# Interleaved token order, two wide stores a step, mirrored x rows gathered by GpSimd, x loaded three steps ahead

## The chip, the core and the metric

The kernel runs on one core of a Trainium2 chip. A core has five engines with queues of their own: PE (TensorE, matmuls; its weight loads are listed as PEld), DVE (VectorE), ACT (ScalarE), POOL (GpSimd) and SP (SyncE, which here only issues DMA transfers). Each engine takes its instructions in order. DMA transfers can be issued from the queues of SP, ACT and POOL. The metric is the device time of one launch, in microseconds (us).

## The reference

What is computed is a Fourier mixing layer (the real part of a 2-D Fourier transform over the 3136 tokens and 256 features), and then a mixer with a low-rank token path and a two-layer channel path:

```python
X = fft(fft(x, axis=1), axis=2).real          # x: 8 x 3136 x 256, float32
h = X.transpose(0, 2, 1) @ U @ V              # U: 3136 x 32, V: 32 x 3136
u = X + h.transpose(0, 2, 1)
out = u + maximum(u @ w_ch1, 0) @ w_ch2       # w_ch1: 256 x 1024, w_ch2: 1024 x 256
```

## The kernel before

The eight batch entries are worked as four pairs. The 3136 tokens are written as n = 64 n1 + n2 on the way in (49 by 64) and as k = 49 k2 + k1 on the way out. Since the input is real, output token k and its mirror are computed together, and so are feature d and 256 - d; only k1 = 0 to 24 is worked, and a mirrored line comes from the same products.

**The input side** of a pair (classes `load_steps`, `s1_steps`): x comes in eight chunks c. `load_pair_chunk` (L96) issues two transfers per chunk from SP's queue: `xa`, 98 rows (2 entries by 49 values of n1) of 4 lines each, and `xb` (L107), the mirrored lines, whose 49 rows of an entry are read in descending order (an access pattern with a negative step, outermost dimension 2). `fold_pair_chunk` (L151, L152) adds the two on POOL into `y`; `fold_pair_chunk_d` and `fold_d` (L141 to L143) fold the features, with two DVE instructions and a small copy of the two edge columns on ACT, into `yb`. Two steps of stage 1 per chunk (L194) multiply `yb` by a table `F`; the result is copied to `z` by ACT and every fourth step stored to DRAM (`zturn`, L206). At the end of the eight chunks `turn` (L274) reads `zturn` back into `g` with another axis on the partitions. `te_steps`, `te_turn`, `te_hidden` and `te_direct` work out the low-rank path (tiles `te`, `TT`, `TE`, `TK`).

**The output side.** `lines` makes eight lines of 64 tokens of one entry from `g` (tile `q`, up to 512 columns at a time); the one row of them that the low-rank product needs is copied into `VZ` by a 1 KB transfer (L383). A pair has 13 chunks of output: 12 with 256 token columns and a mini chunk. A chunk has two steps, so a pair has 26. Per step there are two calls of `mlp1` (L425 and L432 on PE, a copy `ab` on ACT at L435, and two DVE instructions, L438 and L441, that make the hidden tile `hT` and its mirrored twin) for the current chunk, and one `mlp2` with two phases for the chunk before (L480 and the smaller L490 on PE). After the first phase stands a no-operation on ACT (`st.turn`, L492), for which the first matmul of the second phase waits: the two phases write the two halves of a PSUM tile in turned roles. `drain` (L511) copies the result to `om` on ACT, adds and subtracts its halves on POOL into `ob` (L522, L523), and stores `ob` with four transfers of 64 rows of 1 KB (L527).

**The order** is written out by hand in `plan`. `at[n]` holds what is issued in step n of a pair, behind the step's matmuls and ahead of its `drain`. `place_next` places the input side of the next pair: chunk c is loaded at step a + gap c, folded on POOL two steps later, on DVE four, and its stage 1 comes five steps later. `a` and `gap` are 4 and 1.75 in pair 0, and 0 and 2.3 in pairs 1 and 2. Pair 3 has no successor to prepare. Pair 0 also works its own second entry (`turned_steps`, `te_single`) and the tables that are left (`product`, `pair_tables`, `v_lines`, `v_copy`).

**Buffers:** `xa` and `xb` three each, `y` two, `yb` three, `ob` four, `om` three; PSUM has four tiles of two banks, shared by all.

Of the kernel before, what the change touches and what calls it, by code (L numbers as in the profile page):

```python
# [22 lines left out]
def kernel(  # L23
# [19 lines left out]
    ud = nc.dram_tensor("uturn", (NK1, 2, 32, 64), BF16, kind="Internal").ap()  # L43
    x_pn = x.rearrange("b (n1 n2) d -> (b n1) n2 d", n2=N2)
# [28 lines left out]
    sgm = cpool.tile([P, 2], FP32, name="sgm")  # L73
    sg = cpool.tile([P, 2], FP32)
# [21 lines left out]
    def load_pair_chunk(p, c):  # L96
# [10 lines left out]
        nc.sync.dma_start(out=ck.xb.rearrange("p l d -> p (l d)"),  # L107
                          in_=bass.AP(x.tensor, x.offset + r * 4 * D, [[N1 * 64 * D, 2], [-64 * D, N1], [1, 4 * D]]))
# [30 lines left out]
    def fold_d(yb, src, l0, l1):  # L139
        o, i = yb[:, l0:l1, :], src[:, l0:l1, :]  # L140
        nc.vector.tensor_tensor(o[:, :, 1:128], i[:, :, 1:128], i[:, :, 255:128:-1], op=AL.add)  # L141
        nc.vector.tensor_tensor(o[:, :, 129:256], i[:, :, 1:128], i[:, :, 255:128:-1], op=AL.subtract)  # L142
        nc.scalar.copy(o[:, :, 0:129:128], i[:, :, 0:129:128])  # L143
# [32 lines left out]
    def s1_steps(pr, evac):  # L176
# [5 lines left out]
        def step(g):  # L182
# [20 lines left out]
            if g % 4 == 3:  # L203
                lo = max(30 - 2 * g - 1, 0)
                hi = 37 - 2 * g
                nc.sync.dma_start(out=zdp[:, lo:hi, :], in_=z[:, lo:hi, :])  # L206
                if g == 15:
                    nc.sync.dma_start(out=zdp[:, 31, :], in_=z[:, 31, :])
# [76 lines left out]
    def te_turn(pr, bs):  # L285
# [5 lines left out]
        for i, b in enumerate(bs):  # L291
# [3 lines left out]
            copy_act(o[:, :, 64:96], src)  # L295
# [59 lines left out]
    def lines(pr, b, c, evac, now=False):  # L355
# [3 lines left out]
        if now:  # L359
            ps[1] = bank2("ln")  # L360
# [10 lines left out]
    def lines_out(q, ps, b, c, evac, now):  # L371
        c0 = b * 1536 + 512 * c
        o = q[:, :, c0:c0 + 512].rearrange("p k (i s j) -> p s k i j", i=4, s=2)
# [3 lines left out]
        for s in range(2) if now else []:  # L377
            evac[s](o[:, s], ps[s][:, s].rearrange("p (k i j) -> p k i j", k=2, i=4))
            if now:
                evac[s](zr.rearrange("p (i s j) -> p s i j", i=4, s=2)[:, s],  # L380
                        ps[s][64:65, s, 0:256].rearrange("p (i j) -> p i j", i=4))
        if not now:
            nc.sync.dma_start(out=zr, in_=q[64:65, 0, c0:c0 + 512])  # L383
# [27 lines left out]
    def mlp1_parts(ch, u):  # L411
        q, c0, w = ch.pr.q, ch.c0, ch.w
        m = 512 // w
        if u == 0:
            ch.h = hpool.tile([P, 2, JT, 256], BF16, tag="h", name="hT")
# [11 lines left out]
        yield  # L427
        for i in range(m):
# [10 lines left out]
        if not ch.mini:  # L439
            flip = [v.rearrange("p i (t n) -> p (i t) n", n=P) for v in [h[:, 0], a, b]]  # L440
            nc.vector.tensor_tensor(flip[0][:, :, ::-1], flip[1], flip[2], op=AL.max)  # L441
            if u == 0:
# [11 lines left out]
    def mlp2(ch, t, mixed):  # L454
# [56 lines left out]
        def drain(eng):  # L511
# [12 lines left out]
            for i in range(n):  # L524
                for hf, (b, k) in enumerate(ch.units[t]):
                    r = slice(64 - 64 * hf, 128 - 64 * hf) if i else slice(64 * hf, 64 * hf + 64)
                    nc.sync.dma_start(out=out[b].rearrange("(k2 k1) d -> k1 k2 d", k1=N1)[N1 - k if i else k], in_=ob[r, i])  # L527
# [78 lines left out]
    nc.sync.dma_start(out=VZ[96:97].rearrange("p b j -> p (b j)").rearrange("p (a j) -> p a j", j=640), in_=idle[0:5])  # L606
# [119 lines left out]
    nc.gpsimd.memset(V0[:].bitcast(FP32), 0.0)  # L726
    gate = tmp([64, 4], "gate")
# [49 lines left out]
    def v_lines(eng, k0, k1):  # L777
        for r, op in [(0, AL.add), (64, AL.subtract)]:
            o = VZ[r:r + 32, 0, 64 * k0:64 * k1].rearrange("p (k j) -> p k j", j=64)
            eng.tensor_tensor(o, Vk[r:r + 32, k0:k1, :], Vk[r:r + 32, N1 - k0:N1 - k1:-1, ::-1], op=op)  # L780
# [7 lines left out]
    def v_copy(k0, k1, first=True):  # L788
# [29 lines left out]
    bp_sin()  # L818
    te_single(first, 0, teps)
    lps = lines(first, 0, 0, None, now=True)  # L820
    te_turn(first, [0])
    lps([copy_act, copy_dve])
    w1ps = bank2("w1ps")
    w1_fold(1, w1ps)
    te_hidden(first, 0, 0)
    nc.scalar.mul(W1p[1][:], w1ps[:], 0.5)
# [3 lines left out]
    v_copy(1, 9)  # L830
    loads = load_single(1)
# [12 lines left out]
    pairs = [first] + [Pair(p) for p in range(1, NP)]  # L844
    chunks = [ch for p in range(NP) for ch in pair_chunks(p)]
# [12 lines left out]
    def product():  # L858
        ps = bank2("w12")
        for blk in range(2):  # L860
            for j in range(JT):
                nc.tensor.matmul(ps[:, blk, 0:D], W1T[:, j // 4, blk, (j % 4) * P:(j % 4 + 1) * P], W2[:, j, :],
                                 start=(j == 0), stop=(j == JT - 1))
        m = ps[:, :, 0:D]

        copy_act(G[:], m)
        nc.gpsimd.memset(RR[0][0:64].bitcast(FP32), 0.0)
# [164 lines left out]
```

## Time and profile before

| | us |
|---|---|
| median of 2 runs (613.95 to 617.14) | 615.55 |
| the profiled execution | 616.54 |
| its span, first to last instruction | 614.3 |
| PE busy in the span | 485.0 (79%) |
| DVE / ACT / POOL busy | 356.6 / 279.0 / 249.4 |
| mean granted clock of TensorE | 0.875 of full speed |
| moved by DMA | 65.53 MB, 107 GB/s over the span |

In a row of a group, behind the bar, stand the busy time in total and the mean of one instruction in ns, and then the idle time of the engine right before such instructions with what ended it. In a row of a waits view stand the total, the number and the longest of the waits. In a row of a timeline stand start, duration, engine, line and operation, and in brackets the idle time before. In a row of a windows view stand the stretch, its length, the busy time of PE, PEld, DVE, ACT and POOL with the number of instructions, the granted clock, the busy share of the 16 DMA engines and GB/s. In a row of one line's instructions stand the shortest, the median and the longest duration in ns.

### The profile page before, as it was taken

How to read it: one execution, taken by the hardware profiler on the slowest of the kernel's cores; microseconds unless marked ns; L12 is line 12 of the kernel's file. 1: busy time of each engine (PE TensorE's matmuls, PEld its weight loads, DVE VectorE, ACT ScalarE, POOL GpSimd, SP SyncE). 2: the span in 40 equal slices, each digit the busy share in tenths (PEclk: the TensorE clock that was granted, in tenths of full speed). 3: DMA queues.
4: the chain of work that ended last, by engine and by line, in shares of the span. 5: the costliest groups of instructions: out<-in, count | busy, mean ns of one | idle time of the engine just before them, and what ended most of it. 6: DMA issues, size and time to landing. Idle time of an engine off the chain costs nothing. (4 is left out here: it accounts for less than half of the span.)

```text
span 614.3 us, 19104 instructions
## 1 busy us (share of the span) xinstructions
PE 485.0 (79%) x8159; PEld 384.2 (63%) x8159; DVE 356.6 (58%) x592; ACT 279.0 (45%) x505; POOL 249.4 (41%) x342
## 2 busy tenths in 40 slices
PE   4788798294869798886584979878677498999995
PEld 3658575183758476674462847756456285888894
DVE  7567894253764376564465337746456545676673
ACT  5665344152633455353342345534334235656552
POOL 7285334633451234444535124453453512333340
PEclk9788997686978798797795879988869589999998
DMA  8571334444338324334342832443434282233333
GB/s 158 172 106 25 88 110 108 133 117 137 102 109 180 82 91 121 124 100 128 96 126 64 174 88 90 118 130 95 128 93 126 63 180 67 56 75 71 73 80 79
DMA packets 60751, 65.53 MB, mean 107 GB/s; under 512 B 13593, under 2 KB 53496, under 8 KB 60504
## 3 DMA queue, kind: packets, MB, share of 16 engines
q1 hardware_dynamic: 56426, 59.45, 37.2%
q0 software_dynamic: 4160, 4.66, 4.3%
q8 instruction: 63, 1.03, 0.7%
q10 hardware_dynamic: 80, 0.20, 0.1%
q14 instruction: 22, 0.18, 0.1%
HBM read 34.62 MB, written 32.19 MB: 109 GB/s over the span
## 5 line engine op out<-in xcount | busy, mean ns | idle before, releaser
L480 PE MATMUL ops<-W,hT 64*128 64x256 bf16 x3072 | 224.7, 287 | 48.4 <-ACTq L492 41.3
L438 DVE SCALAR_TENSOR_TENSOR hT<-ab,hps 128x512 bf16<-128x512 bf16 x200 | 136.6, 683 | 172.3 <-ACT ab L435 172.2
L480 PEld LDWEIGHTS <-hT 64*128 64x128 bf16 x3072 | 158.9, 100 | 85.7 <-ACTq L492 44.6
L435 ACT CAST ab<-hps 128x512 bf16<-128x512 f32 x200 | 117.0, 590 | 127.1 <-PE hps L432 107.1
L425 PE MATMUL hps<-q,W1p 64*128 64x256 bf16 (+1 forms) x1248 | 131.3, 281 | 13.0 <-DVE hT L441 11.2
L151 POOL TENSOR_TENSOR y<-xa,xb 98x510 f32<-98x510 f32 (+1 forms) x48 | 58.1, 1231 | 192.6 <-DMA xb<-in_x_dram 184.1
L522 POOL TENSOR_TENSOR ob<-om 128x256 f32<-128x256 f32 (+1 forms) x97 | 78.0, 804 | 142.5 <-ACT om L521 121.3
L441 DVE TENSOR_TENSOR hT<-hps,ab 128x512 bf16<-128x512 f32 x192 | 130.8, 681 | 0.0
L425 PE MATMUL hps<-q,W1z 64*128 64x256 bf16 (+1 forms) x416 | 106.3, 282 | 0.0
L432 PE MATMUL hps<-VZ,TE 33*128 33x256 bf16 (+1 forms) x896 | 84.5, 273 | 27.4 <-DMA VZ<-q 27.1
L425 PEld LDWEIGHTS <-W1p 64*128 64x128 bf16 x1248 | 72.9, 99 | 31.0 <-DVE hT L441 19.4
L523 POOL TENSOR_TENSOR ob<-om 128x256 f32<-128x256 f32 (+1 forms) x97 | 78.2, 806 | 0.0
L141 DVE TENSOR_TENSOR yb<-y 98x508 bf16<-98x508 f32 (+1 forms) x24 | 33.8, 1409 | 62.7 <-POOL y L151 62.6
L432 PEld LDWEIGHTS <-TE 33*128 33x128 bf16 x896 | 44.4, 100 | 34.7 <-issue 28.4
L521 ACT COPY om<-ops 128x512 f32<-128x512 f32 (+1 forms) x97 | 56.4, 581 | 9.9 <-PE ops L490 9.8
L490 PE MATMUL ops<-TK,VS 64*128 64x256 f16 x192 | 54.6, 284 | 0.5 <-ACT TK L80 0.5
L425 PEld LDWEIGHTS <-W1z 64*128 64x128 bf16 x416 | 41.0, 99 | 3.0 <-issue 2.1
L490 PEld LDWEIGHTS <-qr 64*128 64x128 bf16 x384 | 38.2, 100 | 3.6 <-issue 0.4
L143 ACT CAST yb<-y 98x8 bf16<-98x8 f32 (+1 forms) x24 | 5.5, 227 | 76.9 <-POOL y L152 76.9
L490 PEld LDWEIGHTS <-q 64*128 64x128 bf16 x384 | 38.2, 100 | 2.8
L490 PE MATMUL ops<-R,qr 64*128 64x256 f16 x192 | 38.9, 284 | 0.0
L490 PE MATMUL ops<-R,q 64*128 64x256 f16 x192 | 38.8, 284 | 0.0
(181 smaller groups left out, 483.0 us busy)
## 6 DMA issues: line engine op xcount, KB each, us to landing
out_dram<-ob SPq DMA_DIRECT2D x392, 64.0 KB
xa<-in_x_dram SPq DMA_DIRECT2D x24, 392.0 KB
xb<-in_x_dram SPq DMA_DIRECT2D x24, 392.0 KB
zturn<-z SPq DMA_DIRECT2D x9, 512.0 KB
g<-zturn SPq DMA_DIRECT2D x6, 416.0 KB
g<-zturn SPq DMA_DIRECT2D x6, 384.0 KB
X<-in_x_dram POOLq DMA_DIRECT2D x4, 384.0 KB, 8.1
X<-in_x_dram POOLq DMA_DIRECT2D x2, 744.0 KB, 8.1
```

Source lines behind the costliest of these rows:

```text
L141: nc.vector.tensor_tensor(o[:, :, 1:128], i[:, :, 1:128], i[:, :, 255:128:-1], op=AL.add)
L151: nc.gpsimd.tensor_tensor(ck.y[:, l0:l1, 1:256], ck.xa[:, l0:l1, 1:256], rb[:, l0:l1, 255:0:-1], op=AL.add)
L425: nc.tensor.matmul(o[s], lt, q[64 * s:64 * s + 64, blk, c0:c0 + w], start=(i == 0 and blk == 0), stop=True, skip_group_check=True)
L432: nc.tensor.matmul(ps[:, s, i * w + a:i * w + a + n], TE[ch.p % 2][b][64 * s:64 * s + 33, ja], VZ[64 * s:64 * s + 33, b, v:v + n], start=F ...
L435: nc.scalar.copy(ab[:], ps[:, 1])
L438: nc.vector.scalar_tensor_tensor(h[:, 1], b, -1.0, a, op0=AL.mult, op1=AL.max)
L441: nc.vector.tensor_tensor(flip[0][:, :, ::-1], flip[1], flip[2], op=AL.max)
L480: mm = nc.tensor.matmul(op, ch.h[rows[half], s, j, t * P:(t + 1) * P], W2[rows[half], j, :], start=(ha == 0 and j == 0), stop=False, skip_ ...
L490: last = nc.tensor.matmul(*g[k], start=False, stop=(k == len(g) - 1), skip_group_check=True)
L521: nc.scalar.copy(om, po)
L522: eng.tensor_tensor(ob[:, 0:n, 0:P], a, om[:, :, 1], op=AL.add)
L523: eng.tensor_tensor(ob[:, 0:n, P:D], a, om[:, :, 1], op=AL.subtract)
```

## The change

- **Token order.** The two lines of a 128-column group are interleaved, token by token, in `q`, `VZ` and the V tiles. The 128 partitions of `ob` are then 64 pairs of neighbouring output rows, and `drain` stores each half of `ob` with one transfer of 128 rows (runs of 2 KB in DRAM): two a step instead of four. The mini chunk stays as it was.
- **xb** is gathered by an indirect DMA from POOL's queue, one row index per partition; the indices are an iota plus an offset, made once.
- **Queues.** `zturn` stores and the `VZ` row transfers are issued from ACT's queue. The edge copy of `fold_d` goes from ACT to DVE.
- **Order.** In `place_next` fold, DVE fold and stage 1 stand one step further behind the load (3, 5, 6); `a` is 3 in pair 0, `gap` 2.25 in pairs 1 and 2.
- **Start.** The first halves of chunk 0's two `mlp1` calls are issued in the preparation. `product` adds the table `Bp` by two matmuls with the identity instead of on DVE; its rows 0 to 63 are filled by POOL and ACT at step 0 (`product_rows`). `v_lines` and `v_zero` all come at step 0, `v_copy`'s mirrored copies go from DVE to ACT. The zero row of `VZ` is a POOL memset instead of a transfer. The copy `qr` is made one `mlp1` call later, and the tile `hT` is taken after the call's first matmuls.

```diff
+    x_g = x.rearrange("b (n1 g l) d -> (b n1 g) (l d)", g=16, l=4)
...
-        r = 2 * p * N1 * 16 + 48 * 16 + 15 - c
-        nc.sync.dma_start(out=ck.xb.rearrange("p l d -> p (l d)"),
-                          in_=bass.AP(x.tensor, x.offset + r * 4 * D, [[N1 * 64 * D, 2], [-64 * D, N1], [1, 4 * D]]))
+        nc.gpsimd.indirect_dma_start(
+            out=ck.xb.rearrange("p l d -> p (l d)"), out_offset=None, in_=x_g,
+            in_offset=bass.IndirectOffsetOnAxis(ap=idx[:, 8 * p + c:8 * p + c + 1], axis=0))
...
-        nc.scalar.copy(o[:, :, 0:129:128], i[:, :, 0:129:128])
+        nc.vector.tensor_copy(o[:, :, 0:129:128], i[:, :, 0:129:128])
...
-                nc.sync.dma_start(out=zdp[:, lo:hi, :], in_=z[:, lo:hi, :])
+                nc.scalar.dma_start(out=zdp[:, lo:hi, :], in_=z[:, lo:hi, :])
                 if g == 15:
-                    nc.sync.dma_start(out=zdp[:, 31, :], in_=z[:, 31, :])
+                    nc.scalar.dma_start(out=zdp[:, 31, :], in_=z[:, 31, :])
...
-        o = q[:, :, c0:c0 + 512].rearrange("p k (i s j) -> p s k i j", i=4, s=2)
+        o = q[:, :, c0:c0 + 512].rearrange("p k (i j s) -> p s k i j", i=4, s=2)
...
-            nc.sync.dma_start(out=zr, in_=q[64:65, 0, c0:c0 + 512])
+            nc.scalar.dma_start(out=zr, in_=q[64:65, 0, c0:c0 + 512])
...
-            for i in range(n):
+            rows = out.rearrange("b (k2 k1) d -> b k2 k1 d", k1=N1)
+            if ch.mini:
                 for hf, (b, k) in enumerate(ch.units[t]):
-                    r = slice(64 - 64 * hf, 128 - 64 * hf) if i else slice(64 * hf, 64 * hf + 64)
-                    nc.sync.dma_start(out=out[b].rearrange("(k2 k1) d -> k1 k2 d", k1=N1)[N1 - k if i else k], in_=ob[r, i])
+                    nc.sync.dma_start(out=rows[b, :, k], in_=ob[64 * hf:64 * hf + 64, 0])
+            else:
+                b, k = ch.units[t][0]
+                for i, k in enumerate([k, N1 - k - 1]):
+                    nc.sync.dma_start(out=rows[b, :, k:k + 2], in_=ob[:, i])
...
-    nc.sync.dma_start(out=VZ[96:97].rearrange("p b j -> p (b j)").rearrange("p (a j) -> p a j", j=640), in_=idle[0:5])
...
+    nc.gpsimd.memset(VZ[96:97].bitcast(FP32), 0.0)
...
-            o = VZ[r:r + 32, 0, 64 * k0:64 * k1].rearrange("p (k j) -> p k j", j=64)
-            eng.tensor_tensor(o, Vk[r:r + 32, k0:k1, :], Vk[r:r + 32, N1 - k0:N1 - k1:-1, ::-1], op=op)
+            o = VZ[r:r + 32, 0, 64 * k0:64 * k1].rearrange("p (i j s) -> p s i j", j=64, s=2)
+            for s in range(2):
+                eng.tensor_tensor(o[:, s], Vk[r:r + 32, k0 + s:k1:2, :], Vk[r:r + 32, N1 - k0 - s:N1 - k1:-2, ::-1], op=op)
...
-            copy_dve(v2[1][0:32, :, ::-1], v2[0][0:32])
-            ts(v2[1][32:64, :, ::-1], v2[0][32:64], -1.0, None)
+            copy_act(v2[1][0:32, :, ::-1], v2[0][0:32])
+            nc.scalar.mul(v2[1][32:64, :, ::-1], v2[0][32:64], -1.0)
...
+    first.u = [mlp1_parts(ch0, i) for i in range(2)]
+    next(first.u[0])
     te_hidden(first, 0, 0)
+    next(first.u[1])
...
+    idx0 = cpool.tile([PR, 8 * NP], I32, name="idx0")
+    nc.gpsimd.iota(idx0[:], pattern=[[PR * 16, NP], [-1, 8]], base=48 * 16 + 15, channel_multiplier=-16)
...
-                                 start=(j == 0), stop=(j == JT - 1))
+                                 start=(j == 0), stop=False, skip_group_check=True)
+        for blk in range(2):
+            nc.tensor.matmul(ps[:, blk, blk * P:(blk + 1) * P], eye[:], Bp[:, blk], start=False, stop=True, skip_group_check=True)
...
-            nc.vector.tensor_tensor(G[:, blk, o], G[:, blk, o], Bp[:, blk], op=AL.add)
-            nc.vector.tensor_tensor(RR[0][64:P, blk, o], RR[0][64:P, blk, o], Bp[64:P, blk], op=AL.add)
-            nc.vector.tensor_copy(RR[0][0:64, blk, o], Bp[0:64, blk])
-            nc.vector.tensor_copy(RR[1][0:64, blk, o], Bp[0:64, blk])
...
-                for o, f in [(0, load), (2, fn), (4, fd), (5, s1[2 * c]), (5, s1[2 * c + 1])]:
+                for o, f in [(0, load), (3, fn), (5, fd), (6, s1[2 * c]), (6, s1[2 * c + 1])]:
                     at[int(a + gap * c) + o].append(f)
-            e = int(a + gap * 7) + 5
+            e = int(a + gap * 7) + 6
...
-            place_next(pairs[1], 4, 1.75)
+            place_next(pairs[1], 3, 1.75)
...
-                place_next(pairs[p + 1], 0, 2.3)
+                place_next(pairs[p + 1], 0, 2.25)
```

More of the change, by code (lines that the diff above doesn't have):

```diff
@@ L73 @@
     sgm = cpool.tile([P, 2], FP32, name="sgm")
+    idx = cpool.tile([PR, 8 * NP], I32)
     sg = cpool.tile([P, 2], FP32)
@@ L427, in mlp1_parts @@
         yield
+        if u == 0:
+            ch.h = hpool.tile([P, 2, JT, 256], BF16, tag="h", name="hT")
         for i in range(m):
@@ L842 @@
     apool = ctx.enter_context(tc.tile_pool(name="apool", bufs=2))
-    pairs = [first] + [Pair(p) for p in range(1, NP)]
-    chunks = [ch for p in range(NP) for ch in pair_chunks(p)]
     NCK = len(chunks) // NP
@@ L985 @@
             n = 2 * (i % NCK) + t
+            if i + t == 0:
+                for g in first.u:
+                    next(g)
+                us_ = []
             if len(us_) == 2:
```

46 lines of the change are left out of this document (26 added, 20 removed).

## The prediction

> **What bounds the kernel now.** I read the busy time by stage first: the windows view, cut at the first matmul of the loop (33.3 us) and at the mini chunk's plain matmuls that close each of the four pairs (206.1, 359, 511.7 and 606.2 us).
>
> ```profile
> core 0: us, PE busy (x) PEld busy (x) DVE busy (x) ACT busy (x) POOL busy (x), PEclk, DMA share, GB/s
> 33.30:94.00 60.70, 50.63 (x991) 41.70 (x992) 47.11 (x101) 29.61 (x55) 31.74 (x44) 0.94 0.39 85
> 94.00:188.00 94.00, 65.80 (x923) 50.80 (x921) 47.86 (x69) 36.64 (x69) 40.83 (x50) 0.78 0.43 121
> 188.00:206.10 18.10, 14.75 (x326) 11.91 (x321) 5.29 (x10) 7.45 (x15) 5.62 (x8) 0.96 0.74 145
> 206.10:359.00 152.90, 119.37 (x1878) 91.14 (x1878) 85.21 (x119) 65.13 (x120) 61.30 (x74) 0.85 0.42 111
> 359.00:511.70 152.70, 119.67 (x1882) 90.96 (x1879) 84.87 (x119) 65.05 (x120) 61.32 (x74) 0.86 0.42 111
> 511.70:606.20 94.50, 91.62 (x1744) 81.57 (x1742) 63.45 (x100) 54.48 (x95) 31.82 (x46) 1.00 0.31 70
> 606.20:614.30 8.10, 1.55 (x12) 0.81 (x10) 1.46 (x5) 0.64 (x2) 0.00 (x0) 0.78 0.36 82
> ```
>
> The last pair prepares no successor: 94.5 us, PE busy for 91.6 of them at clock 1.00, so PE bounds it. Its 26 steps take 94.5/26 = 3.63 us each, a matmul 94.5/1744 = 54 ns. Pairs 1 and 2 issue only 134 more matmuls but take 152.8 us at a clock of 0.85. At 54 ns those would be 7 us; the other 50 us per pair are waiting and the lower clock. What is waited for stands in the groups and the waits (SP's own last):
>
> ```profile
> L480 PE MATMUL ops<-W,hT 64*128 64x256 bf16 x3072 | 224.7, 287 | 48.4 <-ACTq L492 41.3 <-DVE hT L441 5.3 <-DVE hT L438 0.6
> L432 PE MATMUL hps<-VZ,TE 33*128 33x256 bf16 (+1 forms) x896 | 84.5, 273 | 27.4 <-DMA VZ<-q 27.1 <-issue 0.2
> L143 ACT CAST yb<-y 98x8 bf16<-98x8 f32 (+1 forms) x24 | 5.5, 227 | 76.9 <-POOL y L152 76.9
> L151 POOL TENSOR_TENSOR y<-xa,xb 98x510 f32<-98x510 f32 (+1 forms) x48 | 58.1, 1231 | 192.6 <-DMA xb<-in_x_dram 184.1 <-DMA out_dram<-ob 5.8 <-DVE yb L142 2.7
> SPq L527 <- POOL ob L523: 101.9, 46, 12.3
> SPq L527 <- DMA xb<-in_x_dram: 81.3, 18, 5.9
> ```
>
> Read upward, this is one chain. POOL's fold waits 184 us for xb; ACT's edge copy waits for the fold; ACT works in order, so its "bank turn" nop (L492) is late and PE waits 41 us for that. SP's stores, queued behind, wait for xb's transfer too. The timeline of one such stop, and the DMA in its middle:
>
> ```profile
> 107.71 0.57 SPq L103 DMA_DIRECT2D xa<-in_x_dram  x1
> 108.32 0.69 SPq L107 DMA_DIRECT2D xb<-in_x_dram  x1
> 114.68 0.57 SPq L383 DMA_DIRECT2D VZ<-q  x1
> 119.20 2.48 POOL L151 TENSOR_TENSOR y<-xa,xb 98x510 f32<-98x510 f32 x2 [5.55 <-DMA xb<-in_x_dram]
> 120.08 0.61 PE L432 MATMUL hps<-VZ,TE 33*128 33x256 bf16 x4 [11.64 <-DMA VZ<-q]
> ```
>
> ```profile
> 108.40:110.60 2.20, 0.04 (x2) 0.00 (x0) 0.68 (x1) 1.06 (x3) 2.20 (x4) 1.00 0.74 210
> 110.60:111.80 1.20, 0.00 (x0) 0.00 (x0) 1.20 (x2) 0.17 (x1) 1.20 (x2) 1.00 0.13 44
> ```
>
> xa and xb are both 98 rows of 4 KB, 401 KB. For 2.2 us the DMA moves 210 GB/s (462 KB: xa and a start of xb); then only xb is left, at 44 GB/s and a share of 0.13, two of sixteen engines. 401 KB at 44 GB/s are 9.1 us; xb is in use 10.9 us after its issue. The 1 KB row VZ<-q, issued at 114.68, lands 5.4 us later, just when xb is done: it stands behind xb.
>
> **The change, part by part.** *The gather of xb.* One transfer of SP on two engines becomes 98 rows that POOL fetches by index. If they spread as xa's rows do, 401 KB need about 2 us; even the 10.9 us of now would fit in three steps of 3.63 us, which is what the earlier load gives. So I let the 184 us of fold waits go and ask what is late next: the load cycle, 2.25 steps per chunk of x, on the engines it shares.
>
> ```profile
> L438 DVE SCALAR_TENSOR_TENSOR hT<-ab,hps 128x512 bf16<-128x512 bf16 x200 | 136.6, 683 | 172.3 <-ACT ab L435 172.2
> L441 DVE TENSOR_TENSOR hT<-hps,ab 128x512 bf16<-128x512 f32 x192 | 130.8, 681 | 0.0
> L523 POOL TENSOR_TENSOR ob<-om 128x256 f32<-128x256 f32 x94 | 76.8, 817 | 0.0
> L522 POOL TENSOR_TENSOR ob<-om 128x256 f32<-128x256 f32 x94 | 76.6, 815 | 121.9 <-ACT om L521 100.7 <-DMA out_dram<-ob 13.4 <-issue 7.8
> L141 DVE TENSOR_TENSOR yb<-y 98x508 bf16<-98x508 f32 x21 | 25.4, 1208 | 40.5 <-POOL y L151 40.5
> L142 DVE TENSOR_TENSOR yb<-y 98x508 bf16<-98x508 f32 x21 | 23.2, 1105 | 0.0
> L152 POOL TENSOR_TENSOR y<-xa,xb 98x4 f32<-98x4 f32 x21 | 4.4, 210 | 0.0
> L120 POOL DMA_DIRECT2D X<-in_x_dram x6 | 4.1, 685 | 0.3 <-POOL X L114 0.3
> L725 POOL MEMSET TT<- 1x1 bf16 x4 | 0.4, 104 | 0.2
> L780 POOL TENSOR_TENSOR VZ<-uv 32x512 bf16<-32x512 f32 x4 | 8.5, 2122 | 0.1
> 229.20:238.30 9.10, 8.57 (x152) 7.04 (x150) 7.43 (x11) 5.42 (x10) 6.25 (x8) 1.00 0.42 107
> 259.70:271.00 11.30, 9.53 (x177) 7.57 (x173) 8.15 (x12) 6.51 (x12) 7.63 (x9) 1.00 0.41 105
> ```
>
> DVE per cycle: two hT pairs a step, 2.25 x 2 x (0.683 + 0.681) = 6.14, the fold 1.208 + 1.105, and the edge copy that comes over from ACT (0.23 there, I take 0.2): 8.65 us. POOL: drains 2.25 x (0.817 + 0.815) = 3.67, folds 2 x 1.231 + 0.21 = 2.67, and the gather. The trace has no gather. Below stands a plain POOL DMA issue, 0.685; above, 98 indices at the price of POOL's smallest instruction, 98 x 0.104 = 10.2. Nearest is the plain issue, with the index work at the rate of the scattered L780 (2.122/512 = 4.1 ns an element, 0.4 us): 1.1 us, POOL 7.4 us. PE: 2.25 steps x 66 matmuls and 4 of stage 1, 152.5 x 54 ns = 8.2 us. Three engines at 85% and more do not mesh perfectly. The windows of pair 1 hold two stretches at clock 1.00 in which loads, folds and chunks ran nearly unhindered: 152 matmuls in 9.1 us, 177 in 11.3 (9.7 per 152.5). I take their mean, 9.4 us a cycle, with 8.65 and 11.4 as ends (11.4: see the POOL rival).
>
> Pairs 1 and 2: 8 cycles, 75.2; the 8 steps left, 29.1; the about 98 matmuls more than in the last pair that the cycles do not hold (te, lines, turn) at 54 ns, 5.3: 109.6 us each.
>
> *What leaves SP and ACT.* VZ<-q and zturn go to ACT's queue, L143 to DVE. ACT then waits neither for the fold nor, through it, for x; the 41 and 27 us of PE waits go with them (they lie inside the numbers above). The price is 23 + 12 + 3 issues on ACT:
>
> ```profile
> L383 SPq DMA_DIRECT2D VZ<-q x23: 519/554/1187, 37.7 to 564.6; - x23
> L206 SPq DMA_DIRECT2D zturn<-z x12: 532/535/1561, 115.3 to 491.7; - x12
> L527 SPq DMA_DIRECT2D out_dram<-ob x392: 466/594/1925, 54.0 to 611.0; - x196
> 605.91 5.71 SPq L527 DMA_DIRECT2D out_dram<-ob  x9
> ```
>
> At 0.55 us each that is some 7 us a pair on an ACT busy 65 of then 110 us: covered, but each delays the next ab by half a microsecond, and hT, hence PE, waits on ab; without cover up to 7 us a pair (in the upper end). [...] The row of 114.68 shows the queue at work: the issue took 0.57 us, the landing 5.4; but with xb off two engines even a VZ<-q left on SP would land soon, so the sum does not hang on it.
>
> *Stores.* 392 of 64 rows become 200 (192 of 128 rows, 8 mini ones). SP spends 0.594 us on each, 233 us in all; at the same price 119, at double 238, which SP can bear: its stops were waits. At the end the nine stores of 5.7 us become about five: 2 us off the 8.1 (0 to 3).
>
> *Start and pair 0.* The first halves of chunk 0 move forward (about 1 us); the product's additions move from DVE into PE, and the negations of v_copy from DVE to ACT:
>
> ```profile
> 44.88 0.28 PE L315 MATMUL tk<-G,TT 128*32 128x256 f16 x1 [1.69 <-DVE G L873]
> 45.99 0.27 PE L315 MATMUL tk<-G,TT 128*32 128x256 f16 x1 [0.83 <-DVE G L873]
> L555 DVE TENSOR_SCALAR VS<-VS 32x512 bf16<-32x512 bf16 x3 | 3.0, 1010 | 0.1
> ```
>
> That is 2.5 us of PE waiting and 3 us of DVE in a stretch (33.3 to 94) where DVE is busy 78%: with the first item 6.5, so 54 for 60.7. v_lines moves to step 0 as eight half-size POOL instructions, 8.5 us as before, ahead of the first drain: nothing. 94 to 188: 923 matmuls at a cycle's rate (152.5 per 9.4) are 57 for 94. The last 18.1 stay; they hold g's reload, which gets no faster. Pair 0: 129. The interleaved columns of q, VZ and V change strides, not element counts: nothing, at most 10% of a few 1 us copies. The VZ memset, iota and index additions are under 2 us each beside other work.
>
> *Sum:* 33.3 + 129 + 2 x 109.6 + 94.5 + 6.1 = 482 us of span. The profiled execution took 616.54 with a span of 614.3, 2.2 more; so 484. That execution lies 1.0 us above the median of the runs, 615.55; I take that off: **483**.
>
> **The rivals.** *POOL becomes the bound.* The gather is worked out on POOL, beside a DVE that is busier than before. If the gather takes 5 us, POOL's cycle is 3.67 + 2.67 + 5 = 11.4; 24 cycles 2 us longer give 483 + 48 = 531. For it: no row has a gather, and POOL has the least slack of the three. Against: the plain issues, of about as many bytes, cost 0.685. [...]
>
> *ACT takes SP's place.* If a zturn store on ACT is held by full queues as SP's stores were (at most 5.9 us, the SP row above), 12 of them stop ab, hT and PE for 71 us: 554. Against: what filled the queues was xb. For: g's reload keeps a DMA share of 0.74 around it.
>
> *The gather lands no sooner,* because mirrored rows, not two engines, make xb slow. Then it does not do what it says; but with 9.1 us per xb, three ahead and SP free of it, the cycle is still max(9.4, 9.1), with some folds late: about 495. Against: the share of 0.13.
>
> *Slower.* POOL is held for each index, 10.2 us a gather: cycle 16.5, 24 x 7.1 = 170 more: 653. It decides from a cycle of 14.9 (24 x 5.5 = 132 more), a gather of 8.6 us. For it only L725's price per instruction; against it the 0.685.
>
> **How the numbers follow.** Forecast 0.73, POOL 0.09, ACT 0.09, no sooner 0.05, slower 0.03, no change 0.01. Range: the low end is the cycle at 8.65, 24 x 0.75 = 18 less: 465; the high end takes in the gather landing no sooner and reaches POOL's 531: 465 to 531. Faster by over 2% (what a measurement of this kernel can tell) in all but the last two cases: 0.96; same 0.01, slower 0.03.
>
> **What would show it.** L151 with next to no wait for xb; L480 none for ACTq; L432 little for VZ<-q; pairs 1 and 2 near 110 us at clock 0.95 or more; POOL's gathers near 1.1 us; the last pair still 94 us. Wrong would be: gathers over 3 us, L435 or L521 late behind ACT's issues, or a DVE that holds PE for more than 10 us a pair.

## The result, and the profile after

The changed kernel takes **543.14 us** (median of 2 runs, 541.07 to 545.22) where the kernel before takes 615.55: a ratio of 0.8824, with a 95% interval of 0.8649 to 0.8999. The direction was forecast, the size was not: 483 us were predicted, and the range ended at 531. The profiled execution took 545.22 us with a span of 543.4, so the prediction's own sum, 482 us of span, is missed by 61. In the ratios here and below, runs at a clearly lower granted clock are left out, so a ratio is not always the quotient of two medians.

The windows view of the changed kernel, cut as before at the first matmul of the MLP and at the plain matmuls that close each pair (the first halves of two `mlp1` calls now stand ahead of the loop, so the first cut comes earlier):

```profile
core 0: us, PE busy (x) PEld busy (x) DVE busy (x) ACT busy (x) POOL busy (x), PEclk, DMA share, GB/s
...
31.00:181.60 150.60, 126.83 (x2235) 101.03 (x2234) 101.31 (x182) 80.66 (x140) 87.85 (x113) 0.91 0.50 127
181.60:307.30 125.70, 106.25 (x1881) 87.74 (x1879) 84.55 (x128) 67.08 (x112) 67.34 (x82) 0.97 0.46 135
307.30:435.70 128.40, 108.27 (x1881) 88.53 (x1880) 84.75 (x128) 67.28 (x112) 67.09 (x82) 0.96 0.46 132
435.70:537.00 101.30, 92.72 (x1744) 85.15 (x1742) 63.60 (x100) 56.68 (x96) 33.28 (x48) 0.98 0.21 67
```

Every pair is longer than forecast: pair 0 ends at 181.6 us (162 forecast), pairs 1 and 2 take 125.7 and 128.4 (109.6), and pair 3, which loads nothing at all, takes 101.3 where it took 94.5 before. That last one says that the missing time cannot lie in the loads alone. The groups on the page of the same kernel:

```profile
L480 PE MATMUL ops<-W,hT 64*128 64x256 bf16 x3072 | 214.8, 277 | 13.0 <-DVE hT L441 8.5
...
L423 PE MATMUL hps<-q,W1p 64*128 64x256 bf16 (+1 forms) x1248 | 132.1, 276 | 41.7 <-ACT q L82 27.4
...
L432 PE MATMUL hps<-VZ,TE 33*128 33x256 bf16 (+1 forms) x896 | 82.7, 267 | 0.6 <-ACT TE L82 0.6
...
L153 POOL TENSOR_TENSOR y<-xa,xb 98x510 f32<-98x510 f32 (+1 forms) x48 | 58.1, 1229 | 2.4 <-DVE yb L145 2.4
```

What was to go has gone: POOL's fold (L153) waited 184 us for xb and now waits for nothing but 2.4 us of DVE, L480 has lost its 41 us of waiting for ACT but for 2.8, L432 its 27 us for VZ. In their place stands one wait that no rival had: L423, the first matmul of the MLP, waits 27.4 us for ACT's copy of `q`. The waits view counts it, and the timeline of pair 3 shows one of the 18:

```profile
PE hps L423 <- ACT q L82: 27.4, 18, 2.3
```

```profile
456.15 0.27 PE L423 MATMUL hps<-q,W1z 64*128 64x256 bf16 x1
456.15 0.27 PE L423 MATMUL hps<-q,W1p 64*128 64x256 bf16 x1
456.41 1.29 ACT L82 CAST q<-ln 128x1024 bf16<-128x1024 f32 x1 [0.23 <-PE ln L355]
457.75 0.38 PE L423 MATMUL hps<-q,W1p 64*128 64x256 bf16 x3 [1.33 <-ACT q L82]
```

The first two matmuls of a chunk read feature half 0 of `q`, the next read half 1 of the same columns. Those columns have long been there: the copy at 456.41 fills 512 columns of a later chunk, both halves at once. Yet the matmul of half 1 stands still until it is done. It is not the PSUM tile that it waits for either, since the two matmuls before it write the same `hps`. It is a wait without a cause in the data, and it takes up to 2.3 us at each of 18 copies: four or five in each pair, 6.0, 7.0, 7.0 and 7.5 us. The kernel before has the same copy, with the columns in plain order, and hardly such a wait:

```profile
PE hps L425 <- ACT q L80: 0.9, 2, 0.7
```

Which rule makes the two regions count as overlapping when the program is built, no run here shows; only that the interleaved copy of both halves brings the waits.

### The profile page after: what moved, and what is told of

It is laid out like the page before. It is cut to its first block, busy times and chain, and to the rows that moved or that the text cites. A ratio compares the mean times of both kernels' runs of the same rounds, so it can differ in the third digit from the quotient of the medians.

```text
span 543.4 us, 18834 instructions
## 1 busy us (share of the span) xinstructions
PE 455.5 (84%) x8161; PEld 377.4 (69%) x8161; DVE 358.1 (66%) x613; ACT 291.5 (54%) x487; POOL 271.4 (50%) x372
## 4 chain that ended last, share of the span: by engine, by line
PE 54%; DVE 26%; ACT 11%; issue 4%; DMA 2%; POOL 2%; ACTq 1%; DVEq 0%; POOLq 0%
PE ops L480 22%; PE hps L423 12%; DVE hT L441 7%; DVE hT L438 7%; PE hps L432 6%; PE ops L490 5%; ACT q L82 5%; DVE yb L143 4%; ACT ab L435 3%; DVE g L85 3%; DVE yb L144 2%; PE ln L355 2%; DMA w_f<-in_moe_w_ch_dram 1%; PE te L304 1%; PE teps L332 1%
## 5 line engine op out<-in xcount | busy, mean ns | idle before, releaser
L480 PE MATMUL ops<-W,hT 64*128 64x256 bf16 x3072 | 214.8, 277 | 13.0 <-DVE hT L441 8.5
L522 POOL TENSOR_TENSOR ob<-om 128x256 f32<-128x256 f32 (+1 forms) x97 | 71.5, 738 | 234.6 <-ACT om L521 225.4
L480 PEld LDWEIGHTS <-hT 64*128 64x128 bf16 x3072 | 158.4, 96 | 38.6 <-DVE hT L441 16.7
L435 ACT CAST ab<-hps 128x512 bf16<-128x512 f32 x200 | 117.1, 589 | 120.9 <-PE hps L432 115.1
L423 PE MATMUL hps<-q,W1p 64*128 64x256 bf16 (+1 forms) x1248 | 132.1, 276 | 41.7 <-ACT q L82 27.4
L423 PEld LDWEIGHTS <-W1p 64*128 64x128 bf16 x1248 | 72.7, 97 | 58.9 <-issue 34.5
L423 PE MATMUL hps<-q,W1z 64*128 64x256 bf16 (+1 forms) x416 | 104.3, 276 | 0.0
L432 PE MATMUL hps<-VZ,TE 33*128 33x256 bf16 (+1 forms) x896 | 82.7, 267 | 0.6 <-ACT TE L82 0.6
L523 POOL TENSOR_TENSOR ob<-om 128x256 f32<-128x256 f32 (+1 forms) x97 | 73.6, 759 | 0.0
L153 POOL TENSOR_TENSOR y<-xa,xb 98x510 f32<-98x510 f32 (+1 forms) x48 | 58.1, 1229 | 2.4 <-DVE yb L145 2.4
L490 PE MATMUL ops<-TK,VS 64*128 64x256 f16 x192 | 52.8, 275 | 0.5 <-ACT TK L82 0.5
L432 PEld LDWEIGHTS <-TE 33*128 33x128 bf16 x896 | 44.7, 98 | 7.1 <-issue 1.6
L423 PEld LDWEIGHTS <-W1z 64*128 64x128 bf16 x416 | 40.3, 97 | 0.8 <-issue 0.4
L82 ACT CAST q<-ln 128x1024 bf16<-128x1024 f32 (+2 forms) x32 | 32.4, 1025 | 12.4 <-PE ln L355 11.9
L490 PEld LDWEIGHTS <-qr 64*128 64x128 bf16 x384 | 36.9, 96 | 2.4 <-issue 0.4
L490 PEld LDWEIGHTS <-q 64*128 64x128 bf16 x384 | 36.8, 96 | 2.4 <-issue 0.3
L490 PE MATMUL ops<-R,qr 64*128 64x256 f16 x192 | 38.0, 279 | 0.0
L82 ACT CAST z<-s 128x1024 bf16<-128x1024 f32 (+1 forms) x24 | 23.0, 959 | 27.6 <-PE s L196 25.8
L490 PE MATMUL ops<-R,q 64*128 64x256 f16 x192 | 36.6, 271 | 0.0
```

What stands on the lines that cost most here:

```text
L82: nc.scalar.copy(o, i)
L153: nc.gpsimd.tensor_tensor(ck.y[:, l0:l1, 1:256], ck.xa[:, l0:l1, 1:256], rb[:, l0:l1, 255:0:-1], op=AL.add)
L423: nc.tensor.matmul(o[s], lt, q[64 * s:64 * s + 64, blk, c0:c0 + w], start=(i == 0 and blk == 0), stop=True, skip_group_check=True)
L432: nc.tensor.matmul(ps[:, s, i * w + a:i * w + a + n], TE[ch.p % 2][b][64 * s:64 * s + 33, ja], VZ[64 * s:64 * s + 33, b, v:v + n], start=F ...
L435: nc.scalar.copy(ab[:], ps[:, 1])
L480: mm = nc.tensor.matmul(op, ch.h[rows[half], s, j, t * P:(t + 1) * P], W2[rows[half], j, :], start=(ha == 0 and j == 0), stop=False, skip_ ...
```

## The experiments

Times are medians. Each ratio is to the kernel before on the same chip, where that took 618 to 620 us, and carries its 95% interval.

### e1: the copy split by feature half

```diff
-            evac[0](o, ps[0].rearrange("p s (k i j) -> p s k i j", k=2, i=4))
+            for k in range(2):
+                evac[0](o[:, :, k], ps[0].rearrange("p s (k i j) -> p s k i j", k=2, i=4)[:, :, k])
```

> The changed kernel, with the copy of eight lines into q made by two ACT instructions, one for each feature half, instead of one. Theory (a wait that the interleaved copy brings with it, though no data asks for it): in the changed kernel 18 first matmuls of the second feature half wait for the copy of other columns, 27.4 us in all; here that wait falls below 3 us, the copies take 0.65 to 0.75 us each, and the time falls by 20 to 27 us, to 516 to 523 us, a ratio to the kernel before of 0.84 to 0.85. Rival (ACT is simply late, and the wait only shows it): the wait turns up elsewhere, at hT behind ab, and the time stays at 535 to 545 us.

Measured: **513.70 us**, 0.8252 (0.8174 to 0.8329). The copy in the groups by form of the kernel before, of the changed kernel, and of e1:

```profile
L80 ACT CAST q<-ln 128x1024 bf16<-128x1024 f32 x23 | 23.3, 1014 | 12.6 <-PE ln L353 12.6
```

```profile
L82 ACT CAST q<-ln 128x1024 bf16<-128x1024 f32 x23 | 29.9, 1302 | 12.3 <-PE ln L355 11.9
L108 POOL DMA_INDIRECT xb<-in_x_dram,idx x24 | 24.3, 1014 | 4.3 <-issue 2.0 <-POOL ob L523 1.9 <-POOL y L154 0.3
```

```profile
L424 PE MATMUL hps<-q,W1p 64*128 64x256 bf16 x1152 | 120.6, 276 | 18.0 <-DVE hT L442 17.5 <-ACT q L82 0.4
...
L82 ACT CAST q<-ln 128x512 bf16<-128x512 f32 x47 | 31.3, 736 | 9.9 <-PE ln L355 9.8
```

From the changed kernel to e1 ACT's work stays the same (31.3 us for 29.9), the wait falls from 27.4 to 0.4 us, and the span from 543.4 to 513.5. So it was the wait that cost, not the slower copy. The time came out just below the 516 to 523 us expected. (L108 is the gather, for later.) The stages of e1:

```profile
175.80:293.50 117.70, 103.82 (x1880) 83.62 (x1878) 82.17 (x128) 67.09 (x118) 68.24 (x84) 1.00 0.51 145
293.50:411.50 118.00, 105.25 (x1880) 84.47 (x1878) 81.33 (x128) 66.83 (x117) 66.35 (x81) 0.99 0.50 144
411.50:507.00 95.50, 92.06 (x1745) 81.32 (x1742) 63.04 (x100) 56.48 (x101) 33.23 (x48) 1.00 0.21 70
```

Pair 3 is back at 95.5 us. Pairs 1 and 2 are still 8 us over the forecast.

### e2a and e2b: what makes the transfer of xb slow

Both are the kernel before, with xb read from SP in ascending order; the mirror is left out, so the folds add the wrong rows at the same price. e2a keeps an outermost dimension of 2, e2b makes it 98.

```diff
-  [[N1 * 64 * D, 2], [-64 * D, N1], [1, 4 * D]]
+  [[(N1 - 1) * 64 * D, 2], [64 * D, N1], [1, 4 * D]]     # e2a
+  [[64 * D, 2 * N1], [1, 4 * D]]                         # e2b
```

> The kernel before, with the rows of xb read in ascending order (the mirror is left out, so the fold adds the wrong rows), the outermost dimension of the access pattern still 2. Theory (two of sixteen engines): as slow as before; xb alone moves at 40 to 50 GB/s, POOL's folds wait 170 to 200 us for it, 605 to 625 us. Rival (the descending order is what is slow): xb lands in 3 to 4 us, the waits fall below 60 us, 540 to 580 us.

> As the run before it, but with an outermost dimension of 98 rows, as xa has (the mirror is again left out). Theory (two of sixteen engines): the folds' wait for xb falls from 184 us to under 60, and the time to 540 to 575 us with nothing else of the change made. Rival (SP's queue and its order, not the engines, hold xb): the waits stay above 120 us and the time above 590 us.

Measured, one run each: 624.7 us for e2a and 520.39 for e2b, beside 618.8. From the waits of e2a, and then of e2b:

```profile
POOL y L151 <- DMA xb<-in_x_dram: 176.3, 21, 13.8
```

```profile
POOL y L151 <- DMA xb<-in_x_dram: 28.6, 10, 4.8
```

The order of the rows costs nothing that a single run shows; the outermost dimension of 2 costs about 100 us. e2b came out below the 540 to 575 us expected of it. The share of 0.13 in the prediction's rows, taken while xb moved alone, is worth two of the 16 engines (0.13 x 16 = 2.1). That the dimension of 2 is what holds it to two is my reading: these runs show its price, and no row gives the engines of a transfer.

### e4: the gather alone

The kernel before with xb gathered by POOL, loads two steps ahead as they were, and nothing else of the change:

```diff
-        nc.sync.dma_start(out=ck.xb.rearrange("p l d -> p (l d)"),
...
+        nc.gpsimd.indirect_dma_start(
+            out=ck.xb.rearrange("p l d -> p (l d)"), out_offset=None, in_=x_g,
...
```

> The kernel before with the gather of xb from POOL alone: stores, queues, token order and steps (load two steps ahead) as before. Theory (the gather carries the gain): folds wait under 30 us for xb, ACTq and VZ waits of PE under 10 us together, 530 to 565 us. Rival (it takes the ACT queue and the third step as well): a gather that lands too late for two steps keeps over 60 us of fold waits and the time above 585 us.

Measured: **521.93 us**, 0.8430 (0.8347 to 0.8514): faster than the whole change, and below the 530 us that were the least expected. It is also what e2b took (520.39), with a direct transfer of 98 rows and no gather: what the gather brings is what the outermost dimension cost. The rest of the change, taken together, cost some 0.04 of 618, about 24 us; with the copy split it gains, since e1 at 0.8252 lies clear of e4, by 8 to 11 us. From the waits of e4, what is left:

```profile
POOL y L153 <- DMA xa<-in_x_dram: 24.9, 8, 5.5
...
PE hps L434 <- DMA VZ<-q: 11.1, 3, 4.7
```

### e5, e10, e11: the third step

e5 is e1 with xb on SP again as before; e10 is e1, and e11 is e5, with each load issued two steps ahead of its fold and not three:

```diff
-                for o, f in [(0, load), (3, fn), (5, fd), (6, s1[2 * c]), (6, s1[2 * c + 1])]:
+                for o, f in [(1, load), (3, fn), (5, fd), (6, s1[2 * c]), (6, s1[2 * c + 1])]:
```

> The kernel of e1_split_evac (513.7 us) with the mirrored rows fetched by a direct transfer from SP's queue again, three steps ahead, all else kept. Theory (the gather is what ends the fold's waits; the other parts of the change cannot hide a transfer that lands every 10 us or so and holds SP): the fold waits for xb come back, over 100 us of POOL time in all, and the time is 570 to 610 us. Rival (the third step ahead and the two transfers moved to ACT's queue hide the late rows): under 540 us, with under 40 us of such waits.

> The kernel of e1_split_evac (513.7 us) with each load issued two steps before its fold in place of three, the fold where it was. Theory (the gathered rows land in 4.9 us and a step takes over 4 us, so the third step does nothing once the rows are gathered): 511 to 516 us, with under 10 us of POOL waiting for x. Rival (xa, which stands behind the stores in SP's queue, is late with two steps, as in e4_before_gather where POOL waited 24.9 us for it): 518 to 524 us.

> The kernel of e5_split_xb_on_sp (the mirrored rows by a direct transfer from SP; 552 us, 4.2 us of POOL waiting for xb) with the loads two steps ahead in place of three. Theory (the third step is what hid the slow transfer in e5): POOL waits 60 us or more for xb and the time is 575 to 610 us. Rival (what hid it was the freer SP queue, without the turned rows, VZ's rows and half of the stores): 548 to 560 us, with under 20 us of such waits.

Measured: e5 552.16 us, 0.8914 (0.8825 to 0.9003); e10 514.33, 0.8322 (0.8276 to 0.8367); e11 561.74, 0.9074 (0.9030 to 0.9117). From the waits of e5, and then of e11:

```profile
PE ops L481 <- ACTq L493: 20.6, 8, 6.6
...
ACT om L522 <- DMA out_dram<-ob: 14.3, 2, 7.4
...
POOL y L153 <- DMA xb<-in_x_dram: 4.2, 3, 2.9
```

```profile
POOL y L153 <- DMA xb<-in_x_dram: 101.1, 18, 10.8
```

In e5 the fold's waits are as the rival had them and the time is neither's; in e11 the waits are the theory's, and the time again neither's. With three steps the fold hardly waits (4.2 us), with two it waits 101 us: the third step does hide the slow transfer. But that moves the time by 10 us only. Much of what is left stands on ACT. The row that has `om` wait for stores is to be read with care, since `om` is a copy out of PSUM that reads nothing of a store. The timeline of e5 shows what stands right ahead of it:

```profile
130.92 0.53 ACTq L384 DMA_DIRECT2D VZ<-q  x1
131.50 0.59 ACT L522 COPY om<-ops 128x512 f32<-128x512 f32 x1 [7.45 <-DMA out_dram<-ob]
...
131.67 1.89 PE L481 MATMUL ops<-W,hT 64*128 64x256 bf16 x16 [6.64 <-ACTq L493]
```

ACT's own issue of a VZ row is held until a store has landed. ACT works in order, so `om`, the no-operation behind it and with that PE stand for 7 us. Five such stops, four at VZ rows and one at a `zturn` store, come to 24.1 us: 14.3 until stores had landed and 9.8 until xb itself had. This is the mechanism of the prediction's rival "ACT takes SP's place", mostly at the VZ rows. In e1, where xb is off SP, ACT waits for neither. Why the issue has to wait for another transfer, no run here shows.

With the gather (e10 against e1) the third step is worth nothing that can be told: 0.8322 and 0.8252, with intervals that overlap. POOL does wait 14.3 us for gathered rows in e10, more than the 10 expected, but this does not show in the time.

### e6: the start on DVE

In e6, which is e1 otherwise, the memsets and copies of `product_rows` and the first mirrored copies of `v_copy` are DVE's, not POOL's and ACT's.

```diff
-            nc.gpsimd.memset(r[0:64].bitcast(FP32), 0.0)
+            nc.vector.memset(r[0:64].bitcast(FP32), 0.0)
...
-                nc.scalar.copy(r[0:64, blk, blk * P:(blk + 1) * P], Bp[0:64, blk])
+                nc.vector.tensor_copy(r[0:64, blk, blk * P:(blk + 1) * P], Bp[0:64, blk])
...
```

The timeline of the changed kernel shows what they held up:

```profile
42.57 0.90 ACT L890 COPY R<-Bp 64x128 f16<-64x128 f16 x4 [2.13 <-POOL R L888]
...
44.66 1.07 ACT L435 CAST ab<-hps 128x512 bf16<-128x512 f32 x2
...
46.62 1.89 PE L480 MATMUL ops<-W,hT 64*128 64x256 bf16 x16 [3.77 <-DVE hT L441]
```

ACT waits 2.13 us for POOL's memsets and then copies until 44.66, all ahead of `ab`, and PE waits 3.77 us for the `hT` behind it.

> The kernel of e1_split_evac with the memsets and copies of product_rows and the mirrored copies of v_copy put on DVE at the start, in place of POOL and ACT. Theory (at the first step ACT stands behind POOL's memsets and these copies, ahead of the first ab, and PE waits 3.8 us for hT there): the first second-MLP product starts 3 to 5 us sooner, the stage up to the end of pair 0 (175.8 us in e1) shortens by as much, and the time is 508 to 511 us against 513.7. Rival (v_lines on POOL, or the first loads, set the start whichever engine copies): 512 to 515 us, and the wait of PE there is only renamed.

Measured: 508.92 us, 0.8173 (0.8098 to 0.8247). The medians differ as expected but the intervals of e1 and e6 overlap; the traces show the place: the first L491, at 47.5 us in e1, is at 43.2 in e6, and pair 0 ends at 172.1 for 175.8.

### e7: the edge cast back on ACT

```diff
-        nc.vector.tensor_copy(o[:, :, 0:129:128], i[:, :, 0:129:128])
+        nc.scalar.copy(o[:, :, 0:129:128], i[:, :, 0:129:128])
```

> The kernel of e1_split_evac with the narrow edge cast of the fold (402 ns on DVE, once a load step) put back on ACT. Theory (DVE sets the load steps, as the sum of the prediction had it): the stages of pairs 1 and 2 (117.7 and 118.0 us) shorten by 2 to 3 us each, and the time is 506 to 510 us. Rival (ACT, which works in order, stands waiting for the fold at that cast and delivers q and hT late; or PE sets these stages): 513 to 520 us, with more PE waits for ACT.

Measured: 509.43 us, 0.8230 (0.8175 to 0.8285), again an interval that overlaps with e1's. From the windows of e7:

```profile
173.70:289.00 115.30, 103.64 (x1880) 83.74 (x1878) 79.18 (x119) 67.76 (x126) 68.49 (x84) 1.00 0.51 148
289.00:405.30 116.30, 105.20 (x1880) 84.56 (x1878) 79.17 (x119) 67.68 (x126) 67.11 (x81) 0.99 0.51 146
```

DVE has 3.0 and 2.2 us less work in these pairs than in e1, and the pairs are 2.4 and 1.7 us shorter; e9 against e6 makes the same step and gains 1.4 and 1.3 us. Once x comes in time, this copy does not hold ACT up any more (76.9 us in the kernel before, and no such row in the waits of e7), and DVE looks like the engine that lacks the time. These are single profiled executions, and gains this small are not proof.

### e8: the two transfers back on SP

```diff
-                nc.scalar.dma_start(out=zdp[:, lo:hi, :], in_=z[:, lo:hi, :])
+                nc.sync.dma_start(out=zdp[:, lo:hi, :], in_=z[:, lo:hi, :])
...
-            nc.scalar.dma_start(out=zr, in_=q[64:65, 0, c0:c0 + 512])
+            nc.sync.dma_start(out=zr, in_=q[64:65, 0, c0:c0 + 512])
```

> The kernel of e1_split_evac with the transfers of the turned rows z and of VZ's rows issued from SP again, in place of ACT. Theory (on SP they stand behind stores that wait for ob, as in e4_before_gather, where PE waited 11.1 us for VZ and 5.5 us for the turned rows): some 8 to 12 us of such waits return and the time is 520 to 526 us. Rival (moving an issue between engines saves only the issue itself, since the transfers share the same engines; ACT loses 38 issues and is freer): 510 to 515 us.

Measured: 511.82 us, 0.8255 (0.8198 to 0.8312), the same as e1, and in its waits:

```profile
PE hps L433 <- DMA VZ<-q: 2.5, 2, 2.0
```

My theory fell and the rival's 510 to 515 us came. With xb gathered, a VZ row lands in time from either queue: PE waits 1.2 us for one in e1 and 2.5 us in e8. From e1 to e8 the share of the 16 engines that the transfers of SP's queue take rises from 29.8% to 33.3%, and that of ACT's queue falls from 3.3% to 0.2%, so the transfers cost about the same from either. Not even the issue time, 0.52 us for a VZ row on ACT, shows here.

### e9: the two edits together

e1 with the diffs of e6 and of e7.

> The kernel of e1_split_evac with both edits of e6 and e7: the start's copies and memsets on DVE, and the fold's edge cast on ACT. Theory (the two lie in different stages, the start and the load steps, so their gains of 4.8 and 4.3 us add): 503 to 506 us. Rival (each only used up the same slack ahead of the first folds of pair 1): 507 to 510 us.

Measured: **503.37 us**, 0.8120 (0.8089 to 0.8151). That interval is clear of e1's: together the two edits are a gain.

### e12: the gather, the third step and ACT's queue, without the interleaving

e4 with these lines of the change (and the two issues of e8's diff turned to ACT's queue):

```diff
-                for o, f in [(0, load), (2, fn), (4, fd), (5, s1[2 * c]), (5, s1[2 * c + 1])]:
+                for o, f in [(0, load), (3, fn), (5, fd), (6, s1[2 * c]), (6, s1[2 * c + 1])]:
...
-            place_next(pairs[1], 4, 1.75)
+            place_next(pairs[1], 3, 1.75)
...
-                place_next(pairs[p + 1], 0, 2.3)
+                place_next(pairs[p + 1], 0, 2.25)
```

> The kernel of e4_before_gather (before plus the gather, 521.9 us) with the loads three steps ahead and the turned rows and VZ's rows on ACT's queue: the change without the interleaved tokens and their two wide stores, and without its new start. Theory (the interleaving brings nothing that the time shows, since the stores are SP's work and SP is not late once the transfers of two engines are gone): 511 to 516 us, as e1_split_evac. Rival (four stores of 1 KB runs a step keep SP and the transfers behind them late): 518 to 524 us, with POOL still waiting 15 us or more for xa.

Measured: 519.62 us, 0.8362 (0.8315 to 0.8408): the rival's time, but not by its wait. From the waits of e12:

```profile
ACT om L523 <- DMA out_dram<-ob: 7.9, 5, 3.0
...
PE ops L482 <- ACTq L494: 6.6, 5, 2.1
```

POOL's fold hardly waits for xa any more (2.1 us), but ACT's own issues of `zturn` and VZ rows, which stand ahead of `om` as in e5, wait for stores, and PE waits for ACT. In e1, with half as many stores, the first is gone and the second is 1.1 us. So the wide stores look worth a few microseconds. How many is not settled: e12 lacks the new start too, it has the edge copy on ACT, and its interval just touches e1's. It is clear of that of e7 (0.8175 to 0.8285), where the edge copy is on ACT as well.

### e13 and e14: DVE's copies beside POOL's folds

Some 10 us of pair 0 were left over, in a stretch where DVE was busy nearly throughout. The timeline of the kernel before, there, with DVE's copies of the turned rows and POOL's next fold:

```profile
69.58 3.14 DVE L83 COPY g<-zt 32x400 bf16<-32x400 bf16 x8
...
75.35 2.13 DVE L83 COPY g<-zt 32x400 bf16<-32x400 bf16 x8
...
78.06 2.49 POOL L151 TENSOR_TENSOR y<-xa,xb 98x510 f32<-98x510 f32 x2 [6.80 <-DMA xb<-in_x_dram]
```

POOL stood idle for the 6.8 us before that fold, and the group of copies that lies in them takes 2.13. The same copies in e9, with what POOL does beside the second group:

```profile
63.01 5.09 DVE L85 COPY g<-zt 32x400 bf16<-32x400 bf16 x8
...
70.95 6.69 DVE L85 COPY g<-zt 32x400 bf16<-32x400 bf16 x8 [0.35 <-ACT zt L82]
...
71.50 0.83 POOL L523 TENSOR_TENSOR ob<-om 128x256 f32<-128x256 f32 x1 [2.99 <-ACT om L522]
72.29 0.74 POOL L524 TENSOR_TENSOR ob<-om 128x256 f32<-128x256 f32 x1
72.97 1.80 POOL L923 MEMSET UZ<- 128x2048 f32 x1
74.74 2.52 POOL L153 TENSOR_TENSOR y<-xa,xb 98x510 f32<-98x510 f32 x2
```

Eight copies take 2.13 us while POOL is idle and 6.69 while it works. The late rows had kept POOL out of DVE's way; with the gather it is there. e13 gives every second copy to ACT, e14 lets the loads of pair 1 start a step later, both on top of e9:

```diff
-                quarter_rows(g, st.zt, 4 * r - 4, [copy_dve] * 8)
+                quarter_rows(g, st.zt, 4 * r - 4, [copy_act, copy_dve] * 4)     # e13
...
-            place_next(pairs[1], 3, 1.75)
+            place_next(pairs[1], 4, 1.6)                                        # e14
```

> The kernel of e9_split_start_and_edge (503.4 us) with every second copy of the turned rows g of line 1 (16 of 32) on ACT in place of DVE. In e9, two groups of eight such copies take DVE 5.09 and 6.69 us from 63.0 and 71.0 us on, beside POOL's first folds, and 2.13 to 3.14 in the kernel before, where POOL then waited for x. Theory (DVE's copies are slowed by POOL's work beside them, and DVE holds PE there): those two groups shrink to 2 to 4 us of DVE each, pair 0 ends 2 to 5 us sooner than at 168.2, and the time is 498 to 501.5 us. Rival (the copies are slow for another reason, or ACT, 0.5 us a copy, then delays ab by as much): 502.5 to 506 us.

> The kernel of e9_split_start_and_edge with the loads of pair 1 starting a step later and a little closer together (place 4 and 1.6 steps apart in place of 3 and 1.75), so that POOL's first folds move away from DVE's copies of the turned rows. Theory (DVE's copies are slowed by POOL's work): at least one of the two groups of eight copies falls from 5.09 or 6.69 us to under 4, and the time is 499 to 502 us. Rival (the copies stay at 5 us and over where POOL runs beside them or not): 503 to 507 us, as the loads lose a step.

Measured: e13 **498.74 us**, 0.8063 (0.8009 to 0.8116) (the lowest median of all); e14 501.82, 0.8126 (0.8060 to 0.8192). On DVE and PE in e13, and then on DVE in e14:

```profile
64.22 1.06 DVE L85 COPY g<-zt 31x400 bf16<-31x400 bf16 x4
69.56 1.76 DVE L85 COPY g<-zt 31x400 bf16<-31x400 bf16 x4
...
164.00 0.39 PE L499 MATMUL ops<-R,q 128*128 128x256 f16 x2
```

```profile
65.17 3.14 DVE L85 COPY g<-zt 32x400 bf16<-32x400 bf16 x8
70.95 6.69 DVE L85 COPY g<-zt 32x400 bf16<-32x400 bf16 x8
```

In e14 the group that POOL's fold no longer meets falls from 5.09 to 3.14 us, and the other, still beside the memset and a fold, stays at 6.69: the copies follow POOL's work. In e13 pair 0 ends at 164.0 us, 4.2 sooner than in e9, which is near the 162 of the forecast, though by some luck: the MLP starts at 30.1 us and not at 33.3, and pair 0 then takes 133.9 us where 129 were forecast. By the times alone neither e13 nor e14 is to be told from e9, since the intervals overlap; it is the durations of the copies that decide. The two do not simply take turns: copies of 2.13 us that never overlapped with the 5.9 us of POOL's work beside the second group would take 8.0, and they take 6.69. By what mechanism POOL's work slows them, no view shows.

## Why the prediction was right in direction and wrong in size

The span of 482 us against 543.4, taken apart by the runs (each step is a difference of spans): the split copy 29.9 (543.4 to 513.5); start and edge 11.4 (to 502.1 in e9); the turned rows 5.2 (to 496.9 in e13); and 14.9 that remain. The runs of one kernel differ by 4 us and more, so the two smaller steps are rough.

- *"Change strides, not element counts: nothing, at most 10% of a few 1 us copies."* **This is the step that failed.** The copies did get slower, by 28% (1302 ns for 1014), and ACT hid that. What I had not asked is whom the program makes wait for an instruction whose region has changed: 18 matmul groups, 27.4 us of PE, and in all four pairs. The sum put this wait at nothing; e1, which takes it away, is 29.9 us shorter. It should have been among the added waits.
- *The gather at 1.1 us, the fold waits gone.* Right: 1014 ns, and no wait for x. e4 shows that this part alone brings more than the whole gain, and e2a and e2b that what made xb slow was the outermost dimension of 2, not the mirrored rows.
- *"POOL becomes the bound" (531); "ACT takes SP's place" (554); "slower" (653).* None came. POOL issued each gather in 1.0 us, and its folds held ACT up for 1.6 us in all and no other engine. ACT's issues held ACT up for 4.2 us once, and put back on SP (e8) they changed nothing. The argument against that rival, that it was xb which held SP's stores, was right: with xb on SP again (e5, e11) ACT's issues do stand, for 24.1 us in e5. That full queues are what held them was my estimate, and no row shows how full a queue is. That the time lies between the first two is an accident.
- *"The gather lands no sooner" (about 495).* It did not come, as the rows land in 4.9 us. Its price was not tried as it stands, since it has SP free of xb; in e5, which has a slow xb three steps ahead but on SP, the folds hardly wait and the time is still 552, to which the stops of ACT add much.
- *The start: 6.5 us sooner.* It gave nothing, the first L490 being at 49.5 us where it was at 46.7 before. The items I subtracted were real, but what came to POOL and ACT in exchange (memsets, copies) stood ahead of the first `ab`; I had costed `v_lines` and let the rest count as nothing. In e6 the first such matmul comes 4.3 us sooner than in e1.
- *The load cycle, 9.4 us, 8.65 of it DVE.* Most of the 14.9 us lies here: in e13 pairs 1 and 2 take 115.1 and 115.8 us, 5.5 and 6.2 over the forecast. From the windows of e13, pairs 1 to 3:

```profile
164.00:279.10 115.10, 103.82 (x1880) 83.66 (x1878) 79.16 (x119) 67.70 (x127) 68.07 (x82) 1.00 0.51 147
279.10:394.90 115.80, 105.49 (x1880) 84.51 (x1878) 79.17 (x119) 67.92 (x127) 68.18 (x83) 0.99 0.51 147
394.90:490.30 95.40, 91.95 (x1742) 81.27 (x1740) 62.92 (x100) 56.37 (x100) 33.03 (x48) 1.00 0.22 71
```

  PE's work was not priced too low. 54 ns is too little for a stage 1 matmul (at 230.19 us in the kernel before four of them, L194, take 0.62 us, where 16 of L480 take 1.03), but each of the two stretches behind the 9.4 us holds four of them, so their price is in it. Pairs 1 and 2 have 11.9 and 13.5 us more PE work than pair 3, and the forecast had given them 15.1 us more in all. What it lacks is idle time of PE: 11.3 and 10.3 us in pairs 1 and 2, and 3.5 in pair 3. In pair 1 PE waits 8.2 us for DVE (`hT` and `yb`; 3.2 in pair 3) and 2.6 for ACT. So the two stretches meshed better than the cycles do on average, and DVE, which the prediction had as the fullest engine there, is what is mostly waited for. The edge cast was put at 0.2 us a cycle and takes 0.40. All this is read from rows: no run takes these waits away.
- *Pair 0 from 33 to 94 us in 54 us.* The stretch of 78% DVE was seen, but its copies were taken at the durations they had beside an idle POOL. e13 and e14 show why that didn't hold.

## What to carry to other kernels

When a layout changes, ask not only what the copy costs but which instructions must now wait for it: look in the trace for a wait on a producer whose data the waiting instruction does not read, and split that producer along the boundary that its readers use. Where the wait is for a transfer that the waiting instruction does not touch, look at what stands ahead of it in its queue: it can be an issue of a transfer that is held (7.45 us ahead of one copy in e5). When a wait is taken away, what it kept apart can meet, as DVE's copies and POOL's work did here (6.69 us for 2.13), so take durations for the forecast from stretches where the neighbours are busy. And try the parts of a large change one by one: here one of them alone was faster than the whole.

## What the runs showed of the hardware

- With an outermost dimension of 2, the 24 transfers of 98 rows of 4 KB make this kernel about 100 us slower than with one of 98 (624.7 and 520.39 us). The direction of the rows makes no difference that a single run shows (624.7 and 618.8).
- An indirect DMA of 98 rows costs POOL 1.0 us for each issue (0.96 to 1.20 us in e1), and its rows land in 4.9 us (the median in e1). Of the 4.3 us in all that POOL stands idle ahead of the 24 issues, none is put down to DVE.
- An ACT copy of 128 x 1024 from PSUM takes 1302 ns when each run of 64 columns is written to every second one, and 1014 ns when it is written in order.
- A DVE copy of 32 x 400 bf16 takes 0.27 us beside an idle POOL and up to 0.84 beside a busy one (2.13 us for eight in the kernel before, 6.69 in e9).
